# A recurrent attention layer on one core: the maximum subtracted by TensorE, half a of a softmax ahead of half b, and another order at the lead-in

## The chip, the cores and the metric

The kernel runs on one core of a Trainium2 chip. A core has TensorE (PE in the profile; its weight loads are PEld), VectorE (DVE), ScalarE (ACT), GpSimd (POOL) and SyncE (SP), which issues most DMAs. The metric is the device time of one execution in microseconds (us), as the median over several runs.

## The reference

Four layers in the order A, B, A, B, each as `x = x + layer(layernorm(x))`, on 2048 tokens of width 640 in bf16. The change touches layer B alone, a recurrence over 64 segments of 32 tokens with 8 memory tokens, 32 heads of 128:

```python
for s in range(n_seg):                                   # 64 steps, each needs the memory of the one before
    h = jnp.concatenate([mem, xs], axis=1)               # 8 memory rows + 32 tokens
    q, k, v = h @ Wq, h @ Wk, h @ Wv                     # per head, 32 heads of 128
    scores = jnp.where(mask, q @ k.T * scale, -1e9)      # causal among tokens, memory seen by all
    p = softmax(scores)
    o = (p @ v) @ Wo                                     # summed over the heads
    mem = o[:, :8]                                       # the next step's memory
    outs.append(o[:, 8:])
```

## The kernel before

Layer A and layer B follow each other, twice. Everything said here is of `layer_B` (L804). Its instructions are recorded at one line, L113, a wrapper (`_OrdNC`) that chains the instructions of each of TensorE, ScalarE, VectorE and GpSimd in the order of the code: the order written by hand is the order that runs. DMAs go out on SP in the order of the code as well, with eight semaphores in rotation, so that an issue waits for the landing of the eighth before it.

**Rows.** In one step the 32 rows of interest are 24 tokens and the 8 memory rows. `HX` holds their transposed columns; the 24 token columns come from a LayerNorm and a transpose (`ln_spread`, PSUM tile `lntps`) for four steps at a time, and the 8 memory columns are written at the end of the step before, from `MT`. The other 8 tokens of each segment (the "tail") do not depend on the memory; their projections (`TX`, `tail_unit`, `vtail_unit`) are made for four steps at a time and fill TensorE while the recurrence waits. `TK`, `TQ` (tiles `b_tK`, `b_tQ`) hold their K and Q, `VTd` in DRAM their V.

**One step** (from L1086). TensorE makes Ka, Qa, Kb, Qb with `by_head` (20 matmuls of 512 columns, four column tiles at a time; Qb as two passes of 256, `b_Qb` and `b_Qc`). Heads 0 to 15 are half a, 16 to 31 half b. ScalarE copies each to SBUF (`kq`), VectorE transposes (`turn`) into `KT` and `QT`. A mask group starts the PSUM tile of the scores (`mask_mm`, four matmuls of an identity with the mask), `scores` adds 32 small matmuls of a half. Then the softmax: `soft_max` (negated maximum), `soft_sub`, `soft_exp` on ScalarE, `soft_sum`, `soft_rec`, `soft_p` (on GpSimd), and `p_turn` transposes into `PTa` or `PTb`. Va and Vb (`thin_mm`, five chunks of four matmuls each) lie beside it on TensorE. Then come a part of a deferred output product (`OPSd`, from `OTdef`), the tail unit, in some steps `lntps`, then `pv` for half a and half b (PSUM tiles `b_OTP`), evacuated to `OTsb`; two chunks of `vtail`; the output product `OPS` (64 matmuls with the eight tiles `wo`, in the order 0, 4, 1, 5, 3, 7, 2, 6); another part of `OPSd`, `vtail`, and the next memory through `msb` and `MT` into `HX`.

**PSUM.** Five buffers `ps` in rotation, and the pool `po` with one buffer for each of its tags (`tail`, `ops`, `opsd`).

**The lead-in** of a layer B (L996 to L1028) lies at the end of layer A. `load_B_wo` issues the eight `wo` loads on SP, and the dependency with `C.rows` puts layer A's last row stores behind the load with k = 6. Four tail units follow, each with its evacuation and its transpose on VectorE (`tail_turn`, into `b_tK` and `b_tQ`), then the memory: five matmuls into `mt0` and a copy into `HX`, on VectorE too. In SBUF the pools of layer B take the addresses that layer A's tiles leave.

Of the kernel before, what the change touches and what calls it, by code (L numbers as in the profile page):

```python
# [28 lines left out]
D = 640  # L29
# [735 lines left out]
            out_stage_b(nseg - 1, tt)  # L765


class BWeights:
    pass

# [33 lines left out]
def layer_B(nc, tc, C, W, x_src, xb_src, x_dst, mem0, B_Wv, B_Wo, nsteps=64, out_bf16=False, tag=""):  # L804
# [6 lines left out]
    with ExitStack() as ctx:  # L811
        def pool(name, bufs):
            return ctx.enter_context(tc.tile_pool(name=name, bufs=bufs, reuse_waits="tile"))
# [4 lines left out]
        bx = pool("b_x", 1)  # L818
        sml = pool("b_sml", 2)
        kqp = pool("b_kqp", 4)  # L820
        wop = pool("b_wo", 1)
        W.wo = [wop.tile([128, 4, D], BF16, name=f"b_wo{k}") for k in range(7)]
        W.wo.append(pool("b_wo7", 1).tile([128, 4, D], BF16, name="b_wo7"))
        st = pool("b_state", 1)
        w2 = pool("b_w2", 2)
        wk = pool("b_wk", 1)
        sm = pool("b_sm", 2)

# [6 lines left out]
        def ps_tile(shape, dtype, name):  # L835
            return pp.tile(shape, dtype, name=name, tag="ps")
# [2 lines left out]
        Pn = st.tile([128, 2, 5, 64], BF16, name="b_Pn")  # L839
        mask5, selm = C.mask5, C.selm  # L840
        QZ = st.tile([128, 32, 32], BF16, name="b_QZ")
        OTdef = [wk.tile([128, 32, 32], BF16, name=f"b_OTdef{i}") for i in range(2)]

        def init_state():
            XO_ = bx.tile([64, 320], F32, name="b_XO", tag="XO")
            nc.vector.memset(XO_[:], 0.0)
            XOd_ = bx.tile([64, 320], F32, name="b_XOd", tag="XOd")
            nc.vector.memset(Pn[:], 0.0)
            nc.vector.memset(QZ[:], 0.0)
            return XO_, XOd_  # L850
# [4 lines left out]
        def evac(eng, dst, src, scale=None):  # L855
            if eng == "act":
                if scale is None:
                    nc.scalar.copy(dst, src)
                else:
                    nc.scalar.activation(out=dst, in_=src, func=ACT.Copy, scale=scale)  # L860
            else:
                if scale is None:
                    nc.vector.tensor_copy(dst, src)
                else:
                    nc.vector.tensor_scalar(out=dst, in0=src, scalar1=scale, scalar2=None, op0=ALU.mult)
# [27 lines left out]
        def ln_spread(key, ps=None):  # L893
            kind, g = key
            xt = ln_xt.pop(key)
            tps = ps or ps_tile([128, NCH, 4, 32], BF16, "b_lntps")
            for c in range(NCH):
                nc.tensor.transpose(tps[:, c, :, :].rearrange("p i t -> p (i t)"), xt[:, 128 * c:128 * c + 128], C.identb[:])
            if kind == "H":
                HX[g] = hp.tile([128, NCH, 4, 32], BF16, name="b_HX", tag="HX")  # L900
                nc.scalar.copy(HX[g][:, :, :, 0:24], tps[:, :, :, 0:24])
            else:
                TX[g] = tx.tile([128, NCH, 16, 8], BF16, name="b_TX", tag="TX")
                nc.scalar.copy(TX[g][:].rearrange("p c s t -> p c (s t)"), tps[:].rearrange("p c i t -> p c (i t)"))
# [14 lines left out]
        def by_head(cols_ap, Wt, h0, nh, ps):  # L919
            for c in range(NCH):  # L920
                wt = Wt[:, c, 128 * h0:128 * (h0 + nh)].rearrange("p (h e) -> p h e", e=128)
                for j in range(4):
                    nc.tensor.matmul(ps[32 * j:32 * j + 32, :].rearrange("p (h x) -> p h x", x=32), lhsT=cols_ap[:, c, :], rhs=wt[:, :, 32 * j:32 * j + 32],
                                     start=(c == 0), stop=(c == NCH - 1), tile_position=(0, 32 * j), skip_group_check=True)
            return ps
# [4 lines left out]
        def tails_copy(s):  # L930
            g, i = divmod(s, 4)
            KT[s] = wk.tile([128, 32, 40], BF16, name="b_KT", tag="KT")
            for t_, dst in ((TQ, QZ[:, :, 0:8]), (TK, KT[s][:, :, 32:40])):
                nc.gpsimd.tensor_copy(dst, t_[g][:, :, 8 * i:8 * i + 8])
# [11 lines left out]
        def tail_unit(g, k, ps):  # L946
            proj, b = divmod(k, 2)
            return by_head(tail_cols(g), W.wq if proj else W.wk, 16 * b, 16, ps)

        def tail_evac(k, ps):  # L950
            sb = kqp.tile([128, 512], BF16, name="b_tu", tag="kq")
            evac("act", sb[:], ps[:], SCB if k // 2 else None)
            return sb

        def tail_turn(g, k, sb):
            proj, b = divmod(k, 2)
            T_, nm = ((TK, "b_tK"), (TQ, "b_tQ"))[proj]
            if b == 0:
                T_[g] = w2.tile([128, 32, 32], BF16, name=nm, tag=nm)
            nc.vector.transpose(out=T_[g][:, 16 * b:16 * b + 16, :], in_=sb[:].rearrange("p (h x) -> p h x", x=32))  # L960
# [37 lines left out]
        m0 = bx.tile([8, D], BF16, name="b_m0", tag="XOd")  # L998
        nc.sync.dma_start(m0[:], mem0)
        load_B_wv(nc, W, B_Wv)  # L1000
        for k in range(8):
            f = load_B_wo(nc, W, B_Wo, k)
            if k == 6:
                for r in C.rows:
                    tc.add_manual_dep(r.ins, f.ins.name, mybir.DependencyInfo(mybir.DependencyClass.NoSync, mybir.DependencyReason.SCHED_ONLY), reason="order")
        ln_begin(("T", 0), C.after)
        ln_end()
        ln_begin(("H", 0))
        ln_spread(ln_ready.pop(0))
        for k in range(4):  # L1010
            ps = tail_unit(0, k, ps_tile([128, 512], F32, "b_tail"))
            if k == 0:
                ln_end()
                XO, XOd = init_state()
            tail_turn(0, k, tail_evac(k, ps))
        ln_spread(ln_ready.pop(0))
        mt0 = ps_tile([128, NCH, 8], F32, "b_MT0")
        for c in range(NCH):
            nc.tensor.matmul(mt0[:, c, :], lhsT=m0[:, 128 * c:128 * c + 128], rhs=C.identb[0:8, 0:8], start=True, stop=True)
        nc.vector.tensor_copy(HX[0][:, :, 0, 24:32], mt0[:])  # L1020
        tails_copy(0)
        VT[0] = wk.tile([128, 2, 512], BF16, name="b_VT", tag="VT")
        for k in range(4):
            ps = vtail_unit(0, k)
            evac("dve" if k % 2 else "act", VT[0][:, k // 2, 256 * (k % 2):256 * (k % 2) + 256], ps[:])
        for j in range(4):
            nc.sync.dma_start(VTd[1:4].rearrange("s t (b n e) -> (s t) n b e", b=2, e=512)[:, j, :, :], VT[0][32 * j + 8:32 * j + 32, :, :])

# [52 lines left out]
        for s in range(nsteps):  # L1081
# [33 lines left out]
                            nc.tensor.matmul(SP[32 * j:32 * j + 32, 0 if tail else 1 + i, :], lhsT=lhsT, rhs=KT[s][:, h, :],  # L1115
                                             start=False, stop=True, tile_position=(0, 32 * j), skip_group_check=True)

            negmax = sm.tile([128, 2, 5], F32, name="b_negmax", tag="negmax")
            ssum = sm.tile([128, 2, 5], F32, name="b_ssum", tag="ssum")
            rs = sm.tile([128, 2, 5], F32, name="b_rs", tag="rs")  # L1120
            E_ = wk.tile([128, 2, 5, 40], BF16, name="b_E", tag="E0")
# [2 lines left out]
                nc.vector.tensor_reduce(out=negmax[:, b, :], in_=SP[:], axis=AX.X, op=ALU.max, negate=True)  # L1124

            def soft_sub(b, SP):
                nc.vector.tensor_tensor(out=SP[:], in0=SP[:], in1=negmax[:, b, :].unsqueeze(2).to_broadcast([128, 5, 40]), op=ALU.add)

            def soft_exp(b, SP):
                nc.scalar.activation(out=E_[:, b], in_=SP[:], func=ACT.Exp)  # L1130
# [29 lines left out]
                    vps = vtail_unit(work[0], work[1], vc, min(NCH, vc + n_), vps)  # L1160
                    vc = min(NCH, vc + n_)

            VH[s] = wk.tile([128, 2, 512], BF16, name="b_Vth", tag="Vth")
            for b in range(2):
                for nm, Wt, D_, scale in (("K", W.wk, KT, None), ("Q", W.wq, QT, SCB)):
                    if b and nm == "Q":
                        for e, q in enumerate((ps_tile([128, 256], F32, "b_Qb"), po.tile([128, 256], F32, name="b_Qc", tag="tail"))):
                            by_head(cols, Wt, 16 + 8 * e, 8, q)
                            turn(kq(q, scale, 256), D_, 16 + 8 * e, 8)
                    else:  # L1170
                        ps = by_head(cols, Wt, 16 * b, 16, ps_tile([128, 512], F32, f"b_{nm}{'ab'[b]}"))
                        turn(kq(ps, scale), D_, 16 * b, 16)
            SPa = mask_mm(0)
            Va = thin_mm(cols, W.wv, 0, "b_Va", 0, 1)
            scores(0, SPa)
            thin_mm(cols, W.wv, 0, "b_Va", 1, 3, Va)
            SPb = mask_mm(1)
            thin_mm(cols, W.wv, 0, "b_Va", 3, 4, Va)
            scores(1, SPb)
            thin_mm(cols, W.wv, 0, "b_Va", 4, NCH, Va)  # L1180
            PTa = wk.tile([128, 2, 4, 40], BF16, name="b_PTa", tag="PTa")
            PTb = wk.tile([128, 2, 4, 40], BF16, name="b_PTb", tag="PTb")
            soft_max(0, SPa)
            soft_sub(0, SPa)
            soft_exp(0, SPa)
            soft_max(1, SPb)
            soft_sub(1, SPb)
            soft_sum(0)
            soft_rec(0)
            soft_p(nc.gpsimd, 0)  # L1190
            soft_exp(1, SPb)
            evac("act", VH[s][:, 0, :], Va[:])
            soft_sum(1)
            soft_rec(1)
            soft_p(nc.gpsimd, 1)
            p_turn(0, PTa)
            p_turn(1, PTb)
            Vb = thin_mm(cols, W.wv, 1, "b_Vb")
            evac("act", VH[s][:, 1, :], Vb[:])
            if not last:  # L1200
                od_chunk(0)
# [13 lines left out]
            otf = [ps_tile([128, 2, 4, 40] if j else [128, 4, 40], F32, "b_OTP") for j in range(4)]  # L1215
            ots = {j: (otf[j][:, 0, :, :], otf[j][:, 1, :, :]) for j in (1, 2, 3)}
            ots[0] = [otf[0][:], None]
            OTsb = wk.tile([128, 32 * 40], BF16, name="b_OTsb", tag="OTsb")
            OTv = OTsb[:].rearrange("p (a x) -> p a x", a=2)
            pv(0, PTa, ots)  # L1220
            evac("dve", OTv[:, 0, 0:160], otf[0][:].rearrange("p i c -> p (i c)"))
# [156 lines left out]
```

## Time and profile before

| | |
|---|---|
| median of three runs | 2438.76 us (2437.13 to 2443.8) |
| the profiled execution: its time, its span | 2441.25 us, 2439.1 us |
| granted TensorE clock, mean over the span | 0.993 |
| TensorE, weight loads | 2296.4 us (94%), 1507.5 us (62%) |
| VectorE, ScalarE, GpSimd | 1882.4, 1414.9, 749.2 us |
| first `Ka` of the two layers B | 360.15 and 1580.78 us |
| a step of layer B, median of 90 without and 36 with `lntps` | 13.19 and 13.24 us |
| the first step of each layer B | 15.95 and 14.93 us |

The times of instructions come from the profiled execution, and "busy" is the time in which an engine has an instruction in work. A row of a group gives line, engine, operation, output<-input by the names of the program, the tile shapes, the count, then busy us, mean ns of one, and the idle time ahead of them with what ended most of it. A row of the timeline gives start, duration of the whole stretch (all its instructions together), engine, line, and in brackets an idle time with what ended it. Durations of matmuls include their pipeline, so the spacing of the groups gives their cost.

### The profile page before, as it was taken

What the parts mean: (1) busy time and instruction counts of PE and PEld (TensorE: products, weight loads), DVE (VectorE), ACT (ScalarE), POOL (GpSimd) and SP (SyncE); (2) the same over time, 40 slices, a digit from 0 to 9 for tenths busy, and PEclk for the clock granted to TensorE, in tenths of its full rate; (3) what the DMA queues carried; (4) which work ended last, traced back from release to release, by engine and by line L of the source; (5) the groups of instructions that cost most, each with busy time, mean ns of one, the idle gap of its engine ahead of it and who ended that gap; (6) DMA issues with size and microseconds to landing.
All of it is one profiled execution on the core that took longest, in us unless ns stands there. A gap on an engine that the chain in (4) does not pass through costs nothing.

```text
span 2439.1 us, 139382 instructions
## 1 busy us (share of the span) xinstructions
PE 2296.4 (94%) x62322; PEld 1507.5 (62%) x62386; DVE 1882.4 (77%) x4699; ACT 1414.9 (58%) x3194; POOL 749.2 (31%) x1589
## 2 busy tenths in 40 slices
PE   8999989999999999999889999899999999999998
PEld 5566656666666666666555666566666666666665
DVE  8999857777777777777679998577777777777776
ACT  6999954444454444444369899544444544444443
POOL 5677631111111111111146776311111111121111
PEclk9999999999999999999999999999999999999999
DMA  4121271111111111111220111711111111111110
GB/s 166 49 82 62 70 258 24 28 32 29 31 29 30 30 30 31 30 31 27 66 86 18 66 40 37 270 23 26 28 27 29 28 25 27 27 29 26 29 24 19
DMA packets 168883, 123.38 MB, mean 51 GB/s; under 512 B 104652, under 2 KB 153180, under 8 KB 166492
## 3 DMA queue, kind: packets, MB, share of 16 engines
q1 hardware_dynamic: 167288, 112.69, 16.1%
q8 instruction: 487, 7.98, 1.4%
q10 hardware_dynamic: 996, 1.79, 0.2%
q14 instruction: 112, 0.92, 0.1%
HBM read 79.60 MB, written 34.80 MB: 47 GB/s over the span
## 4 chain that ended last, share of the span: by engine, by line
PE 66%; DVE 15%; ACT 10%; DMA 4%; issue 2%; POOL 1%; SPq 1%; ACTq 0%; DVEq 0%; POOLq 0%
PE b_OPS L113 11%; PE b_Ka L113 6%; PE b_Qa L113 5%; PE b_Kb L113 5%; DVE a_nm L142 4%; ACT a_PT L142 4%; PE b_Va L113 4%; PE b_Vb L113 4%; PE b_tail L113 4%; PE b_vtail L113 3%; PE a_S L113 3%; PE b_OTP L113 2%; PE b_OPSd L113 2%; PE b_SP L113 2%; PE b_Qb L113 2%
## 5 line engine op out<-in xcount | busy, mean ns | idle before, releaser
L113 PEld LDWEIGHTS <-b_HX 128*32 128x32 bf16 x17920 | 466.4, 96 | 287.4 <-DVE b_HX L113 17.4
L113 POOL TENSOR_TENSOR b_Pn<-b_E,b_rs 128x200 bf16<-128x200 bf16 x256 | 133.5, 522 | 1096.4 <-DVE b_rs L113 1078.5
L142 DVE TENSOR_REDUCE a_nm<-a_S 128x2 f32<-128x512 f32 (+3 forms) x512 | 395.4, 817 | 54.6 <-PE a_S L113 39.1
L142 ACT ACTIVATE a_PT<-a_T 128x1024 bf16<-128x1024 f32 (+1 forms) x384 | 345.9, 905 | 28.7 <-PE a_T L113 21.8
L113 PE MATMUL b_OPS<-b_wo,b_OTsb 128*32 128x320 bf16 x8192 | 307.0, 301 | 4.5 <-DVE b_OTsb L113 4.5
L113 PEld LDWEIGHTS <-b_OTsb 128*32 128x32 bf16 x8192 | 207.4, 97 | 74.7 <-DVE b_OTsb L113 27.0
L113 DVE STREAM_TRANSPOSE b_KT<-b_kq 128x512 bf16<-128x512 bf16 x256 | 181.3, 708 | 84.6 <-ACT b_kq L113 83.9
L142 POOL TENSOR_SCALAR_AFFINE_SELECT a_PT<-a_PT 128x256 bf16<-128x256 bf16 x380 | 188.5, 501 | 158.3 <-ACT a_PT L142 157.0
L113 ACT ACTIVATE b_E<-b_SP 128x200 bf16<-128x200 f32 x256 | 86.3, 337 | 235.1 <-DVE b_SP L113 224.1
L113 PE MATMUL b_Va<-b_wv,b_HX 128*32 128x512 bf16 x2560 | 221.9, 381 | 0.0
L113 DVE STREAM_TRANSPOSE b_QT<-b_kq 128x256 bf16<-128x256 bf16 (+1 forms) x384 | 183.9, 504 | 39.9 <-ACT b_kq L113 36.5
L113 DVE CAST b_HX<-b_MT 128x16 bf16<-128x16 f32 (+1 forms) x380 | 65.0, 172 | 185.7 <-PE b_MT L113 177.5
L113 ACT CAST b_msb<-b_OPS 128x64 bf16<-128x64 f32 x378 | 69.3, 256 | 210.9 <-PE b_OPS L113 210.9
L113 PE MATMUL b_Ka<-b_wk,b_HX 128*32 128x512 bf16 x2560 | 165.1, 385 | 14.6 <-DVE b_HX L113 14.4
L113 PEld LDWEIGHTS <-b_TX 128*32 128x32 bf16 x5360 | 143.5, 96 | 55.6 <-issue 2.8
L113 DVE CAST b_OTsb<-b_OTP 128x160 bf16<-128x160 f32 (+1 forms) x384 | 133.9, 376 | 43.7 <-PE b_OTP L113 39.4
L113 PE MATMUL b_Qa<-b_wq,b_HX 128*32 128x512 bf16 x2560 | 162.6, 383 | 0.0
L113 PE MATMUL b_Vb<-b_wv,b_HX 128*32 128x512 bf16 x2560 | 162.3, 379 | 0.0
L113 PE MATMUL b_Kb<-b_wk,b_HX 128*32 128x512 bf16 x2560 | 161.5, 381 | 0.0
L113 ACT CAST b_kq<-b_Ka 128x512 bf16<-128x512 f32 x128 | 74.9, 585 | 133.6 <-PE b_Ka L113 133.6
L113 PE MATMUL b_vtail<-b_wv,b_TX 128*32 128x256 bf16 x2680 | 148.8, 273 | 1.2 <-issue 1.2
L113 ACT CAST b_OTsb<-b_OTP 128x320 bf16<-128x320 f32 x256 | 96.5, 429 | 82.2 <-PE b_OTP L113 81.1
(186 smaller groups left out, 5049.5 us busy)
## 6 DMA issues: line engine op xcount, KB each, us to landing
b_wv<-in_B_Wv_dram SPq DMA_DIRECT2D x10, 1024.0 KB
b_wo<-in_B_Wo_dram SPq DMA_DIRECT2D x16, 640.0 KB
b_VT<-b_VTd SPq DMA_DIRECT2D x504, 16.0 KB
b_XO<-xres SPq DMA_DIRECT2D x256, 30.0 KB
b_VTd<-b_vt SPq DMA_DIRECT2D x480, 16.0 KB
b_xt<-xres_bf SPq DMA_DIRECT2D x40, 160.0 KB
b_wk<-in_B_Wk_dram SPq DMA_DIRECT2D x20, 256.0 KB
b_wq<-in_B_Wq_dram SPq DMA_DIRECT2D x20, 256.0 KB
```

The costliest lines, as they stand in the source:

```text
L113: r = f(*a, **k)
L142: r = f(*a, **k)
```

## The change

1. `soft_sub` is four matmuls (slices of the identity with the negated maximum broadcast over 40 columns) that add into the PSUM tile of the scores; `negmax` is bf16.
2. Qb is one pass of 512 columns in a `ps` buffer. Its transpose follows `soft_max` of half a on VectorE.
3. On TensorE, scores a follow mask a at once; then three chunks of Va, the subtraction of half a, the rest of Va, mask b, scores b, two chunks of Vb, the subtraction of half b, the rest of Vb. On VectorE, sum a and reciprocal a stand ahead of maximum b, and the transpose of `PTa` ahead of sum b. The product P of half b is made by VectorE.
4. At the lead-in, five `wo` loads stand ahead of layer A's last row stores and the other three behind later loads. The copy of the memory stands ahead of the four transposes of the tail units, and `init_state` behind them. ScalarE makes all four evacuations of V.
5. The pools are laid out anew: `b_w2` and `b_state` ahead of `wo`, `wo` in two pools, and `OTdef`, `Vth`, `PTa`, `PTb`, `OTsb` in a pool `b_wkl`.

```diff
+WO_FIRST, WO_LAST = (0, 4, 1, 5, 3), (7, 2, 6)
...
-        wop = pool("b_wo", 1)
-        W.wo = [wop.tile([128, 4, D], BF16, name=f"b_wo{k}") for k in range(7)]
-        W.wo.append(pool("b_wo7", 1).tile([128, 4, D], BF16, name="b_wo7"))
+        w2 = pool("b_w2", 2)
         st = pool("b_state", 1)
-        w2 = pool("b_w2", 2)
+        W.wo = [None] * 8
+        for nm, ks in (("b_wo", WO_FIRST), ("b_wol", WO_LAST)):
+            p_ = pool(nm, 1)
+            for k in ks:
+                W.wo[k] = p_.tile([128, 4, D], BF16, name=f"b_wo{k}")
+        wkl = pool("b_wkl", 1)
         wk = pool("b_wk", 1)
...
-        for k in range(8):
+        for k in WO_FIRST + WO_LAST:
             f = load_B_wo(nc, W, B_Wo, k)
-            if k == 6:
+            if k == WO_FIRST[-1]:
...
         ln_spread(ln_ready.pop(0))
+        tsb = []
         for k in range(4):
             ps = tail_unit(0, k, ps_tile([128, 512], F32, "b_tail"))
+            tsb.append(tail_evac(k, ps))
             if k == 0:
                 ln_end()
-                XO, XOd = init_state()
-            tail_turn(0, k, tail_evac(k, ps))
...
         nc.vector.tensor_copy(HX[0][:, :, 0, 24:32], mt0[:])
+        for k in range(4):
+            tail_turn(0, k, tsb[k])
+        XO, XOd = init_state()
...
-            evac("dve" if k % 2 else "act", VT[0][:, k // 2, ...], ps[:])
+            evac("act", VT[0][:, k // 2, ...], ps[:])
...
-            negmax = sm.tile([128, 2, 5], F32, name="b_negmax", tag="negmax")
+            negmax = sm.tile([128, 2, 5], BF16, name="b_negmax", tag="negmax")
...
             def soft_sub(b, SP):
-                nc.vector.tensor_tensor(out=SP[:], in0=SP[:], in1=negmax[:, b, :].unsqueeze(2).to_broadcast([128, 5, 40]), op=ALU.add)
+                for j in range(4):
+                    nc.tensor.matmul(SP[32 * j:32 * j + 32], lhsT=C.identb[:, 32 * j:32 * j + 32], rhs=negmax[:, b, :].unsqueeze(2).to_broadcast([128, 5, 40]),
+                                     start=False, stop=True, tile_position=(0, 32 * j), skip_group_check=True)
...
+                    ps = by_head(cols, Wt, 16 * b, 16, ps_tile([128, 512], F32, f"b_{nm}{'ab'[b]}"))
+                    sbs = kq(ps, scale)
                     if b and nm == "Q":
-                        for e, q in enumerate((ps_tile([128, 256], F32, "b_Qb"), po.tile([128, 256], F32, name="b_Qc", tag="tail"))):
-                            by_head(cols, Wt, 16 + 8 * e, 8, q)
-                            turn(kq(q, scale, 256), D_, 16 + 8 * e, 8)
+                        qb = sbs
                     else:
-                        ps = by_head(cols, Wt, 16 * b, 16, ps_tile([128, 512], F32, f"b_{nm}{'ab'[b]}"))
-                        turn(kq(ps, scale), D_, 16 * b, 16)
+                        turn(sbs, D_, 16 * b, 16)
             SPa = mask_mm(0)
-            Va = thin_mm(cols, W.wv, 0, "b_Va", 0, 1)
             scores(0, SPa)
-            thin_mm(cols, W.wv, 0, "b_Va", 1, 3, Va)
-            SPb = mask_mm(1)
-            thin_mm(cols, W.wv, 0, "b_Va", 3, 4, Va)
-            scores(1, SPb)
-            thin_mm(cols, W.wv, 0, "b_Va", 4, NCH, Va)
             soft_max(0, SPa)
+            turn(qb, QT, 16, 16)
+            Va = thin_mm(cols, W.wv, 0, "b_Va", 0, 3)
             soft_sub(0, SPa)
             soft_exp(0, SPa)
-            soft_max(1, SPb)
-            soft_sub(1, SPb)
+            thin_mm(cols, W.wv, 0, "b_Va", 3, NCH, Va)
+            SPb = mask_mm(1)
+            scores(1, SPb)
             soft_sum(0)
             soft_rec(0)
             soft_p(nc.gpsimd, 0)
+            soft_max(1, SPb)
+            evac("act", VH[s][:, 0, :], Va[:])
+            Vb = thin_mm(cols, W.wv, 1, "b_Vb", 0, 2)
+            soft_sub(1, SPb)
             soft_exp(1, SPb)
-            evac("act", VH[s][:, 0, :], Va[:])
+            thin_mm(cols, W.wv, 1, "b_Vb", 2, NCH, Vb)
+            p_turn(0, PTa)
             soft_sum(1)
             soft_rec(1)
-            soft_p(nc.gpsimd, 1)
-            p_turn(0, PTa)
+            soft_p(nc.vector, 1)
             p_turn(1, PTb)
-            Vb = thin_mm(cols, W.wv, 1, "b_Vb")
             evac("act", VH[s][:, 1, :], Vb[:])
```

## The prediction

> **What bounds the kernel now.** I read the page first: the shares by engine, then the chain that ended last.
>
> ```profile
> PE 2296.4 (94%) x62322; PEld 1507.5 (62%) x62386; DVE 1882.4 (77%) x4699; ACT 1414.9 (58%) x3194; POOL 749.2 (31%) x1589
> PE 66%; DVE 15%; ACT 10%; DMA 4%; issue 2%; POOL 1%; SPq 1%; ACTq 0%; DVEq 0%; POOLq 0%
> ```
>
> TensorE is busy for 94% of the span and carries two thirds of the chain. A wait that disappears from another engine is therefore worth little unless TensorE stands for it, and anything added to TensorE is suspect. The list of waits says who stands where (summed us, count, mean us):
>
> ```profile
> ACT b_E L113 <- DVE b_SP L113: 224.1, 248, 2.3
> PE b_Ka L113 <- DVE b_HX L113: 14.4, 4, 7.7
> PE b_OTP L113 <- DVE b_PTb L113: 10.3, 33, 0.6
> ```
>
> ScalarE's 224 us before the exponentials is idle time of an engine that has time. TensorE itself waits inside the softmax only at its end (the P·V matmuls of half b, on `PTb`), and twice for long at a lead-in (`Ka` on `HX`). Next, the timeline of a step without a LayerNorm transpose; its first `Ka` matmul is at 735.53, and all offsets below count from there (start, us, engine):
>
> ```profile
> 735.53 1.26 PE L113 MATMUL b_Ka<-b_wk,b_HX 128*32 128x512 bf16 x20
> ...
> 739.87 0.26 PE L113 MATMUL b_SP<-b_mask,c_identb 128*32 128x200 bf16 x4
> ...
> 741.47 0.38 DVE L113 TENSOR_TENSOR b_SP<-b_SP,b_negmax 128x200 f32<-128x200 f32 x1
> 741.59 1.27 PE L113 MATMUL b_Vb<-b_wv,b_HX 128*32 128x512 bf16 x20
> ...
> 743.71 0.57 DVE L113 STREAM_TRANSPOSE b_PTa<-b_Pn 128x256 bf16<-128x256 bf16 x2
> 744.29 0.57 DVE L113 STREAM_TRANSPOSE b_PTb<-b_Pn 128x256 bf16<-128x256 bf16 x2
> 744.33 0.20 PE L113 MATMUL b_OTP<-b_PTa,b_Vth 32*128 32x40 bf16 x4
> ...
> 744.79 0.33 DVE L113 CAST b_OTsb<-b_OTP 128x160 bf16<-128x160 f32 x1
> 745.01 0.20 PE L113 MATMUL b_OTP<-b_PTb,b_Vth 32*128 32x40 bf16 x4 [0.30 <-ACT b_tu L113]
> 745.32 0.40 PE L113 MATMUL b_vtail<-b_wv,b_TX 128*32 128x256 bf16 x8
> ```
>
> From `Ka` to the end of the tail unit (8.49) TensorE never stands. Then P·V a starts at 8.80, just after `PTa` ends (8.75), and P·V b at 9.48, 0.15 after `PTb` ends (9.33). The steps last 13.19 us (median of 90 without `lntps`) and 13.24 (36 with it). A step with `lntps`, whose `Ka` is at 709.15, has no such slack:
>
> ```profile
> 717.75 0.45 PE L113 MATMUL b_lntps<-c_identb,b_xt 128*128 128x128 bf16 x5
> 718.14 0.20 PE L113 MATMUL b_OTP<-b_PTa,b_Vth 32*128 32x40 bf16 x4
> 718.60 0.32 DVE L113 CAST b_OTsb<-b_OTP 128x160 bf16<-128x160 f32 x1
> 718.97 0.40 PE L113 MATMUL b_vtail<-b_wv,b_TX 128*32 128x256 bf16 x8
> ```
>
> P·V a follows TensorE's own work there (8.99). `vtail` takes the PSUM buffer that the CAST empties, so it comes 0.83 to 0.84 after P·V a (9.83).
>
> **The step, part by part.** *The maximum on TensorE.* Two DVE subtractions of 0.375 go. Two groups of four 128x200 matmuls come; the mask group before is the same form, and the next group starts 0.09 after it (739.87, 739.96): +0.18 on TensorE.
>
> *Q b in one pass.* The 512 columns cost what twice 256 cost (1.08 each by the spacing of the groups): nothing. But half b's `QT` now needs one ScalarE cast of 0.60 and one DVE transpose of 0.71 in place of two halves that overlap.
>
> *Scores b.* Q b ends at 4.33, its cast ends at 5.20, `QT` b runs 5.24 to 5.95 (max a stands ahead of it, 4.86 to 5.23, behind `KT` b). TensorE meanwhile does mask a and scores a (to 4.64), Va (1.08), subtraction a, mask b: to 5.92. Scores b can start at 6.01: +0.09 waited.
>
> *Subtraction b.* Subtraction a is over at 5.40, ScalarE starts 0.27 later (as the CAST does behind P·V a, 718.34 to 718.60) and exp a, 0.34, ends at 6.01; DVE does sum a and rec a (6.04 to 6.60) ahead of max b (6.55 to 6.92), so subtraction b starts at 6.98. TensorE has finished scores b at 6.23 and two of the five chunks of Vb at 6.67: +0.31 waited. Were max b free of the two, it would still take 0.18 until the last score is out of the array, 0.37 for the reduction and 0.10 for two hand-overs, less 0.44 of cover: 0.21. The eight `Vb` matmuls of 0.055 are the whole cover, and behind the waiting matmul stand the rest of Vb, OPSd and the tail unit, which need no softmax at all. I charge both waits in full because every group of matmuls in the timeline stands in the order of the code. The Trainium skill ("TensorE: Matmul & The Clock Gate", step by step) says that only weight loads are pulled ahead and matmuls keep their order, which speaks against this change; if matmuls could overtake, 0.18 alone would be added. No row of before decides that alone.
>
> *Half a ahead of half b.* `PTa` ends about 7.87 in place of 8.75. Half b's chain: exp b 7.34 to 7.68, then `PTa`, sum b, rec b, P b on DVE (0.38 by the subtraction's row, POOL took 0.522), `PTb` 8.80 to 9.37, P·V b not before 9.52. So `PTb` hardly comes earlier than now: DVE wins 0.75 of subtractions and gives back 0.38 and the wait on TensorE.
>
> *Sum.* TensorE reaches the P·V stage 0.18 + 0.09 + 0.31 = 0.58 later: 9.07, and 9.19 with the 0.12 that the change of matmul form takes now. Without `lntps` P·V a goes 8.80 to 9.19 and `vtail` 9.19 + 0.84 = 10.03 in place of 9.79: +0.24, as slack absorbs 0.34. With `lntps` nothing absorbs it: P·V a 9.57, `vtail` 10.41, +0.57. So 90 x 0.24 + 36 x 0.57 = 42.1, and 0.6 for the two last steps: +42.7 us. Bounds for TensorE's addition are 0.43 (no wait on `QT`, 0.25 on the maximum) and 0.68 (0.1 more in hand-overs): steps +0.09 and +0.41, or +0.34 and +0.66, so +23 to +55.
>
> **The two lead-ins.** Here the change removes a wait. The first:
>
> ```profile
> 357.52 1.30 DVE L113 STREAM_TRANSPOSE b_tK<-b_tu 128x512 bf16<-128x512 bf16 x2 [4.02 <-DMA xres<-a_xnew]
> ...
> 359.94 0.16 DVE L113 CAST b_HX<-b_MT 128x40 bf16<-128x40 f32 x1
> 360.15 0.62 PE L113 MATMUL b_Ka<-b_wk,b_HX 128*32 128x512 bf16 x4 [5.48 <-DVE b_HX L113]
> ```
>
> The CAST that `Ka` needs stands behind four transposes, whose targets lie in memory that layer A's last row stores still read. TensorE idles 5.5 us here and 7.7 in the second lead-in. Ahead of the transposes, and with their targets moved, the CAST needs only its matmuls: `Ka` starts when `vtail` ends, 354.7 and 1573.2. The windows show what else goes (PEclk is third from the end):
>
> ```profile
> 354.70:360.00 5.30, 0.00 (x0) 0.00 (x0) 2.48 (x5) 0.00 (x0) 0.00 (x0) 0.93 0.88 285
> 360.20:366.30 6.10, 6.10 (x60) 2.25 (x64) 1.98 (x4) 1.18 (x2) 0.74 (x2) 0.52 0.18 40
> ```
>
> After the idling the granted clock is 0.52 for 6.1 us. The first steps take 15.95 and 14.93 where a usual one takes 13.19: 2.8 and 1.7 more. The gain is 5.5 + 2.8 + 7.7 + 1.7 = 17.7 us. The Trainium skill (same page, what is actually happening) has half clock until one busy window of 3.4 us: as an estimate from it 1.7 us a lead-in, and 16.6 in all; the row of 6.1 us is longer, so the rows decide. Three weights (`wo` 7, 2, 6, 640 KB each) now queue on SP behind `b_xt`, `XOd` and `XO`. The first of them is used by the sixth of the eight groups of the first OPS, 10.0 + 1.4 us after `Ka`, at 366 and 1584.6; at the 285 GB/s of the window their 1.9 MB take 6.9 us, to about 361 and 1583. The TensorE work of the first step is the cover; without it each late us is paid. ScalarE takes two evacuations from DVE (0.37 each) under the step's start: nothing.
>
> Net: 42.7 - 17.7 = +25.0. The profiled execution took 2441.25 us (span 2439.1), so 2466.3; it lies 2.5 above the median of the three runs, so against 2438.76: **2464 us**.
>
> **Rivals.**
> *A, the end of softmax still ends the step (faster).* If the two new waits together stay under 0.16, TensorE comes at most 0.34 late, P·V b still waits for `PTb` (9.52 against 9.48), and the 90 steps lose nothing; 36 lose 0.18 to 0.34, 6.5 to 12. Net -11 to -5: 2428 to 2433, likeliest 2430. For it: `PTb` is what P·V b waits for now. Against: max b behind the long `QT` b, sum a and rec a, all in rows above. This is also the result if a waiting matmul lets others pass.
> *B, the lead-ins win nothing (slower still).* The late weights or the stores hold the first OPS by some 9 us in each lead-in: +42.7 is left, 2481. For: the DMA share is 0.88. Against: 11 us of TensorE work in between.
> *C, the two parts cancel.* The steps cost only 11 to 25 us, at or below the low bound, the lead-ins give 17.7: 2432 to 2446.
>
> **How the numbers follow.** The forecast has 0.66, A 0.17, B 0.08, C 0.09. The forecast's own range is 2464 with the steps' bounds and a lead-in gain of 13 (no help from the clock) to 18: 2444 to 2481. The range of 8 in 10 takes in C and B with a little over: 2436 to 2486; what lies outside is A and the low end of C. Some 0.3%, 7.3 us, is what a measurement can tell from no change. Faster: most of A, 0.14. Within: the rest of A and C, 0.12. Slower: the forecast and B, 0.74.
>
> **What would show it.** Right: steps of about 13.43 and 13.81; `vtail` 10.03 and 10.41 after `Ka`; new rows of waits of TensorE's `b_SP` on `b_negmax` (about 40 us) and on `b_QT` (about 11); no row of ScalarE waiting for DVE's `b_SP`; `Ka` at 354.7 with a granted clock near 1.0 and first steps near 13.4. Wrong: subtraction b starts within 0.1 of the second Vb chunk, or P·V b still waits for `PTb` in most steps (A); OPS of the first steps waits for a DMA (B).

## The result, and the profile after

The changed kernel takes 2466.3 us (median of four runs, 2463.69 to 2470.78) beside 2437.95 us; the ratio is 1.0108, 95% interval 1.0092 to 1.0125. The forecast was 2464. The profiled execution took 2463.69 us with a span of 2462.0, 22.9 more than the span before.

The page after, shares by engine and the chain:

```profile
PE 2340.5 (95%) x60850; PEld 1470.0 (60%) x60850; DVE 1829.7 (74%) x4439; ACT 1431.8 (58%) x3070; POOL 683.4 (28%) x1461
PE 69%; DVE 16%; ACT 9%; issue 3%; DMA 3%; SPq 1%; POOL 0%; ACTq 0%; DVEq 0%; POOLq 0%
```

VectorE gave up 53 us of work and TensorE took on 44 us of busy time. TensorE's share of the chain rose from 66% to 69%. The waits of TensorE in layer B (summed us, count, longest us; the prediction calls the third column a mean, which it is not, but no step of its sum uses it as one):

```profile
PE b_SP L113 <- DVE b_negmax L113: 11.1, 58, 0.4
PE b_Ka L113 <- DVE b_HX L113: 4.6, 5, 1.6
...
PE b_OTP L113 <- issue: 3.9, 2, 2.3
PE b_OTP L113 <- DVE b_PTb L113: 2.4, 8, 0.3
```

The wait for `PTb` has gone from 10.3 to 2.4 us, the one at the lead-ins from 14.4 to 4.6, and a wait for the maximum has come in their place. The trace before has 55 more waits of the P·V matmuls that the prediction's list leaves out, put down to the copy that ends together with `PTb`; they are gone too:

```profile
PE b_OTP L113 <- ACT b_tu L113: 16.5, 55, 0.3
```

A step without `lntps`, `Ka` at 749.78:

```profile
754.69 0.37 DVE L113 TENSOR_REDUCE b_negmax<-b_SP 128x5 bf16<-128x200 f32 x1
754.97 0.71 DVE L113 STREAM_TRANSPOSE b_QT<-b_kq 128x512 bf16<-128x512 bf16 x1
755.11 0.27 PE L113 MATMUL b_SP<-b_negmax,c_identb 128*32 128x200 bf16 x4
...
755.95 0.63 PE L113 MATMUL b_Vb<-b_wv,b_HX 128*32 128x512 bf16 x8
...
756.35 0.33 DVE L113 TENSOR_REDUCE b_negmax<-b_SP 128x5 bf16<-128x200 f32 x1
756.73 0.27 PE L113 MATMUL b_SP<-b_negmax,c_identb 128*32 128x200 bf16 x4
756.82 0.83 PE L113 MATMUL b_Vb<-b_wv,b_HX 128*32 128x512 bf16 x12
...
758.61 0.57 DVE L113 STREAM_TRANSPOSE b_PTb<-b_Pn 128x256 bf16<-128x256 bf16 x2
758.93 0.20 PE L113 MATMUL b_OTP<-b_PTa,b_Vth 32*128 32x40 bf16 x4
```

Two chunks of Vb cost 0.44 by their spacing, so the subtraction of half b could stand at 756.39 and stands at 756.73, right behind the reduction: 0.34 lost. The bar of the Vb matmuls (0.63) hides half of that, since it includes the pipeline; the profile counts only 21.9 us of idle time ahead of all the subtraction's matmuls, where the spacing ahead of half b alone gives about 0.34 x 126 = 43. P·V a comes at offset 9.15. In a step with `lntps` (`Ka` at 763.12) it comes at 9.53:

```profile
772.65 0.20 PE L113 MATMUL b_OTP<-b_PTa,b_Vth 32*128 32x40 bf16 x4
...
773.49 0.40 PE L113 MATMUL b_vtail<-b_wv,b_TX 128*32 128x256 bf16 x8
```

Where the 22.9 us come from, by the first `Ka` of each step in both traces (us):

| | before | after | difference |
|---|---|---|---|
| start to the first `Ka` | 360.15 | 352.91 | -7.2 |
| first steps of the two layers | 15.95, 14.93 | 15.62, 16.20 | +0.9 |
| last `Ka` of the first layer B to first of the second | 378.19 | 369.53 | -8.7 |
| the other 2 x 62 steps | 1651.0 | 1687.6 | +36.6 |
| last step and the rest | | | +1.2 |

The 88 steps without `lntps` among them went from 13.19 to 13.44 in the median (mean 13.31 to 13.48), the 36 with it from 13.24 to 13.72 (mean 13.33 to 13.93).

Not all of the first and third row belongs to the change. In the trace before, TensorE's granted clock was 0.50 for 3.4 us in the midst of each layer A, from 116.9 and from 1396.9 us (first fence; the columns are us, then busy us of PE, PEld, DVE, ACT, POOL, then clock, DMA share, GB/s). The trace after has full clock there (second fence) and runs 1.6 and 1.4 us further ahead from there on, in code that the change does not touch:

```profile
116.90:120.30 3.40, 3.18 (x16) 1.33 (x13) 2.86 (x5) 2.17 (x4) 3.00 (x8) 0.50 0.20 62
```

```profile
116.90:120.30 3.40, 3.25 (x36) 1.67 (x35) 3.40 (x7) 3.14 (x6) 3.01 (x8) 1.00 0.22 71
```

Why the clock fell there is not known; the traces of other runs have such a stretch at other places of layer A, or none. Without these 3.0 us the traces are 25.8 us apart, and the ratio of the run times gives 26.

### The profile page after: what moved, and what is told of

Read it like the earlier page. It is cut to its first block, busy times and chain, and to the rows that moved or that the text cites. A ratio compares the mean times of both kernels' runs of the same rounds, so it can differ in the third digit from the quotient of the medians.

```text
span 2462.0 us, 135749 instructions
## 1 busy us (share of the span) xinstructions
PE 2340.5 (95%) x60850; PEld 1470.0 (60%) x60850; DVE 1829.7 (74%) x4439; ACT 1431.8 (58%) x3070; POOL 683.4 (28%) x1461
## 4 chain that ended last, share of the span: by engine, by line
PE 69%; DVE 16%; ACT 9%; issue 3%; DMA 3%; SPq 1%; POOL 0%; ACTq 0%; DVEq 0%; POOLq 0%
PE b_OPS L113 11%; PE b_Ka L113 6%; PE b_Kb L113 5%; PE b_Qa L113 5%; PE b_Qb L113 5%; PE b_tail L113 5%; DVE a_nm L142 5%; PE b_vtail L113 4%; ACT a_PT L142 4%; PE b_SP L113 4%; PE b_Va L113 3%; PE b_Vb L113 3%; PE b_OPSd L113 3%; PE a_S L113 3%; PE b_OTP L113 2%
## 5 line engine op out<-in xcount | busy, mean ns | idle before, releaser
L113 PEld LDWEIGHTS <-b_HX 128*32 128x32 bf16 x15360 | 385.2, 96 | 277.8 <-DVE b_HX L113 7.2
L113 POOL TENSOR_TENSOR b_Pn<-b_E,b_rs 128x200 bf16<-128x200 bf16 x128 | 66.8, 522 | 985.6 <-ACT b_Vth L113 897.6
L113 PEld LDWEIGHTS <-b_OTsb 128*32 128x32 bf16 x8192 | 236.7, 97 | 44.0 <-DVE b_OTsb L113 7.7
L113 PEld LDWEIGHTS <-c_identb 128*32 128x32 bf16 (+1 forms) x3032 | 155.4, 96 | 176.4 <-issue 103.5
L113 DVE STREAM_TRANSPOSE b_QT<-b_kq 128x512 bf16<-128x512 bf16 x256 | 180.8, 706 | 37.9 <-ACT b_kq L113 34.0
L113 PEld LDWEIGHTS <-b_TX 128*32 128x32 bf16 x5360 | 151.3, 96 | 62.8 <-issue 0.8
L113 PE MATMUL b_Vb<-b_wv,b_HX 128*32 128x512 bf16 x2560 | 186.9, 380 | 0.0
L113 PE MATMUL b_Va<-b_wv,b_HX 128*32 128x512 bf16 x2560 | 180.2, 380 | 0.0
L113 PE MATMUL b_Qb<-b_wq,b_HX 128*32 128x512 bf16 x2560 | 160.6, 379 | 0.0
```

Of the source, the lines that this page charges most:

```text
L113: r = f(*a, **k)
```

## The experiments

**The lead-in alone.**

The change without its items 1 to 3: everything from `negmax` on in the diff above is taken back, among it

```diff
-            thin_mm(cols, W.wv, 1, "b_Vb", 2, NCH, Vb)
...
-            p_turn(0, PTa)
             soft_sum(1)
             soft_rec(1)
-            soft_p(nc.vector, 1)
+            soft_p(nc.gpsimd, 1)
+            p_turn(0, PTa)
             p_turn(1, PTb)
+            Vb = thin_mm(cols, W.wv, 1, "b_Vb")
```

> The new lead-in, pools and order of the weights, with the step as it was before (subtraction on VectorE, Qb in two passes, old order, both products P on GpSimd). My theory: the change is the sum of a gain at the two lead-ins (about 15 us by the trace after: first Ka 7.2 and 8.7 us earlier, the first steps about as long as before) and a loss in the steps. So 2438 - 15 = 2423 us, ratio 0.994, steps at 13.19 and 13.24, first Ka at 352.9. Rival: the lead-in wins nothing by itself and the steps cost only what the total shows, 28 us: then about 2438.

Measured: ratio 0.9965 (0.9953 to 0.9976), some 8 us less than before; first `Ka` at 352.75, gap 367.97, first steps 16.19 and 16.22, the other steps 13.22 and 13.23. The lead-in gains by itself, so the rival falls, but by the run times it gains little more than half of the 15 us expected. The traces show where the rest went. First `Ka`, gap and first steps are 16 us shorter than before, but 3.0 of these are the clock in layer A, which is 1.00 there in this trace too. The 124 other steps sum to 4 us more than before, in single long steps (15 of them above 13.6 us, where before has 12); in five of the 15 TensorE stands for 0.3 us or more at what the profile calls `issue`, which is explained under the run without the late weights. That leaves about 9 us. Against this kernel the changed step costs 1.0108/0.9965 = 1.0144, 35 us.

**More cover ahead of the subtraction of half b.**

```diff
-            Vb = thin_mm(cols, W.wv, 1, "b_Vb", 0, 2)
+            Vb = thin_mm(cols, W.wv, 1, "b_Vb", 0, 4)
             soft_sub(1, SPb)
             soft_exp(1, SPb)
-            thin_mm(cols, W.wv, 1, "b_Vb", 2, NCH, Vb)
+            thin_mm(cols, W.wv, 1, "b_Vb", 4, NCH, Vb)
```

> The changed kernel with four chunks of Vb, in place of two, ahead of the subtraction of half b. My theory: TensorE's wait for the maximum of half b (0.28 in every step) is what the steps pay beyond the slack. The subtraction comes at about 7.04 in place of 6.95, nothing waits for it, TensorE reaches P V a at 8.84 in place of 9.15, P V b stays on PTb at 9.5; steps 13.22 and 13.44 in place of 13.44 and 13.72, so 90 x 0.22 + 36 x 0.28 = 30 us less: 2436, ratio 0.999. Rival: half b's chain on VectorE (sum, reciprocal, P, PTb) sets the step already, the wait on TensorE is hidden: 2466, or more as exp b comes 0.1 later.

Measured: ratio 1.0037 (1.0023 to 1.0051), 17 us less than the changed kernel where 30 were expected. P·V a came at 8.81 in place of 9.15, as worked out, and the wait moved on:

```profile
PE b_OTP L113 <- DVE b_PTb L113: 33.1, 88, 0.6
```

88 waits for `PTb` in place of 8: half b's chain on VectorE now ends the step (P·V b at 9.54). Steps took 13.34 and 13.47; the second is as expected, the first loses 0.1 more than I gave it. The wait on TensorE was real and worth something, and close behind it stood a second bound.

**The same, with P of half b on GpSimd again.**

```diff
-            soft_p(nc.vector, 1)
+            soft_p(nc.gpsimd, 1)
```

> The run with four chunks of Vb ahead of the subtraction of half b, and the product P of half b on GpSimd (0.522 and two hand-overs) in place of VectorE (0.38). My theory: with the wait on TensorE gone, half b's chain to PTb ends the steps without lntps (P V b at 9.54, waiting on PTb in most steps), so 0.25 to 0.3 longer is paid there nearly in full and less with lntps: 88 x 0.25 + 36 x 0.07 = 25 us more than with VectorE, ratio 1.014. Rival: TensorE's own work still ends the steps there: 1.0037 as it was.

Measured: ratio 1.0137 (1.0115 to 1.0159), where 1.014 was expected; 122 waits for `PTb`, 66.4 us in all. That half b's chain is the bound there is shown.

**The subtraction back on VectorE, the rest as changed.**

```diff
-                for j in range(4):
-                    nc.tensor.matmul(SP[32 * j:32 * j + 32], ...)
+                nc.vector.tensor_tensor(out=SP[:], in0=SP[:], in1=negmax[:, b, :]..., op=ALU.add)
```

> The changed kernel with the subtraction back on VectorE (two of 0.375 us per step, f32 maximum), everything else as changed. My theory: TensorE loses its 0.18 of matmuls and its wait, but VectorE's chain, which is as long as TensorE's in the changed order, gets 0.75 longer and sub a stands behind QT b: PTb ends at about 10.2 in place of 9.4, P V b 10.3, vtail 10.6: steps +0.55 without lntps and +0.25 with it, 58 us more: 2524, ratio 1.035. Rival: the matmuls on TensorE are the whole loss: then 0.49 less per step where it counts, about 2420 to 2440.

Measured: ratio 1.0322 (1.0307 to 1.0338). The wait tells why:

```profile
PE b_OTP L113 <- DVE b_PTb L113: 109.2, 120, 1.1
```

In the new order the subtraction on VectorE is worse: TensorE's matmuls save 2% there. So the matmuls are not what is wrong with the change.

**Maximum b ahead of sum a and reciprocal a.**

```diff
+            soft_max(1, SPb)
             soft_sum(0)
             soft_rec(0)
             soft_p(nc.gpsimd, 0)
-            soft_max(1, SPb)
```

> The changed kernel with maximum b ahead of sum a and reciprocal a on VectorE, nothing else. My theory: TensorE's wait shrinks by 0.1 (subtraction b at 6.85 in place of 6.95, the floor being scores b, the reduction and two hand-overs), but VectorE stands idle from 5.95 until the scores of half b are there and everything behind (sum a, P a, PTa, sum b, P b, PTb) comes 0.6 to 0.7 later: P V b at 10.2 in place of 9.55, steps +0.45 without lntps, +0.2 with it: 47 us more, 2510 to 2520, ratio 1.030. Rival: only TensorE's wait counts: 0.1 x 124 = 12 us less, ratio 1.006.

Measured: ratio 1.0351 (1.0336 to 1.0367), a little more than expected. The subtraction of half b moved from 6.95 to 6.86 in the steps with `lntps`, as worked out, and P·V b from 9.55 to 10.2 or 10.3, waiting for `PTb` 125 times. In this order neither place of maximum b is good: half b's scores come 0.34 later than before (5.95 in place of 5.61), and either VectorE waits for them ahead of half a's work, or TensorE waits behind that work. How much of these 0.34 comes from Qb in one pass, and how much from Va ahead of them, no run separates.

**The subtraction on TensorE in the old order.** Lead-in as in the first experiment, maxima back to back as before (the main lines against that experiment; the comments are not in the code, and the later line of Vb goes):

```diff
             soft_max(0, SPa)
             soft_sub(0, SPa)          # four matmuls, behind the last chunk of Va
             soft_exp(0, SPa)
             soft_max(1, SPb)
+            Vb = thin_mm(cols, W.wv, 1, "b_Vb", 0, 2)
             soft_sub(1, SPb)          # four matmuls
+            thin_mm(cols, W.wv, 1, "b_Vb", 2, NCH, Vb)
```

> The new lead-in with the old order of the step (Qb in two passes, maximum b right behind maximum a, P b on GpSimd), but the subtraction as four matmuls on TensorE: of half a behind the last chunk of Va, of half b behind two chunks of Vb. My theory: the matmuls alone cost 0.18 where TensorE is the bound, and the loss of the change is the order on VectorE (sum a and reciprocal a ahead of maximum b, with too little cover). Here the maxima end at 5.91 and 6.28, both subtractions find them ready, PTb ends about 0.13 earlier: steps without lntps -0.13, with it +0.18, so 88 x -0.13 + 36 x 0.18 = -5 us against the lead-in alone: ratio 0.9945. Rival: the subtraction on TensorE is itself the loss (hand-overs between the engines included): steps +0.2 to +0.3 in all, +30 us, ratio 1.009.

Measured: ratio 0.9927 (0.9912 to 0.9943), faster than both kernels and, a little more than the 0.9945 expected, than the lead-in alone. Steps 13.08 and 13.39 in the median, against 13.22 and 13.23 of the lead-in alone: -0.14 and +0.16, worked out as -0.13 and +0.18. A step with `Ka` at 888.56:

```profile
894.39 0.41 PE L113 MATMUL b_Va<-b_wv,b_HX 128*32 128x512 bf16 x4
894.62 0.27 PE L113 MATMUL b_SP<-b_negmax,c_identb 128*32 128x200 bf16 x4
894.66 0.37 DVE L113 TENSOR_REDUCE b_negmax<-b_SP 128x5 bf16<-128x200 f32 x1 [0.19 <-PE b_SP L113]
894.70 0.62 PE L113 MATMUL b_Vb<-b_wv,b_HX 128*32 128x512 bf16 x8
...
895.14 0.27 PE L113 MATMUL b_SP<-b_negmax,c_identb 128*32 128x200 bf16 x4
```

The subtraction of half b stands 0.44 behind the start of Vb: no wait. The same eight `Vb` matmuls are enough cover here, because the reduction starts with Vb (894.66 and 894.70), where in the changed kernel it starts 0.40 later (756.35 and 755.95).

**TensorE's subtraction only where there is slack.**

```diff
+            on_dve = bool(ln_ready)
...
             def soft_sub(b, SP):
+                if on_dve:
+                    nc.vector.tensor_tensor(out=SP[:], in0=SP[:], ...)
+                    return
                 for j in range(4):
```

> The version with the old order and the subtraction on TensorE, but in the 36 steps with a LayerNorm transpose the subtraction stays on VectorE. My theory: with lntps TensorE has no slack before P V a, so the 0.18 of matmuls are paid in full there (13.39 against 13.23), and are hidden, with an earlier PTb, in the others (13.08 against 13.22). So 36 x 0.16 = 6 us less than with TensorE everywhere: ratio 0.990, steps 13.08 and 13.23. Rival: the steps with lntps are longer for what the step before or the transpose itself brings: no difference, ratio 0.9927.

Measured: ratio 0.9897 (0.988 to 0.9915), steps 13.04 and 13.23. `ln_ready` is true in the steps that make `lntps`; the maximum is f32 there. By ratio that is 7 us less than with TensorE everywhere, though the two intervals overlap a little; by the steps the 0.16 is won back. It is the lowest ratio of this study.

**Without the late weights.**

```diff
         for k in WO_FIRST + WO_LAST:
+            if k in WO_LAST:
+                W.wo[k] = W.wo[WO_FIRST[WO_LAST.index(k)]]
+                continue
             f = load_B_wo(nc, W, B_Wo, k)
```

> The changed kernel without the loads of the three late weights: output products of the head groups 7, 2 and 6 use the tiles 0, 4 and 1, so those products are left out and others stand in their place. My theory: TensorE's stalls inside the first steps (2.3 us, and 1.6 + 1.2 us with a clock of 0.67 after) come from these three transfers, which fill the DMA queues until the first P V and beyond; without them the first steps take about 13.5 in place of 15.6 and 16.2, 4.8 us less: 2461, ratio 1.009. Rival: the stalls come from the first pass through the step's code whatever the queues carry: first steps 15.6 and 16.2 as they are, 2466.

The kernel leaves out three of the eight weights: their products use tiles 0, 4 and 1. Measured: ratio 1.0057 (1.004 to 1.0075), 12 us less than the changed kernel (5 were expected), and first steps of 13.28 and 13.18. By the traces the first steps give 5.4 us, about as expected; the other 4.7 us of their difference lie between the layers and in the other steps, and their cause is not shown. That the three transfers lengthen the first steps is shown. What they do there is seen in the changed kernel's own trace: TensorE stands within one group of P·V b, whose other matmuls of the same inputs have run, and the row says `issue`: it waits for nothing that the profile shows.

```profile
365.05 0.19 PE L113 MATMUL b_OTP<-b_PTb,b_VT 8*128 8x40 bf16 x1 [2.29 <-issue]
```

```profile
1593.85 0.19 PE L113 MATMUL b_OTP<-b_PTb,b_VT 8*128 8x40 bf16 x2 [1.57 <-issue]
```

The windows (us, PE, PEld, DVE, ACT, POOL, clock, DMA share, GB/s) show the queues full when the stall begins, and empty at that time in the kernel without these loads (second fence):

```profile
361.00:363.00 2.00, 1.47 (x79) 0.77 (x71) 1.55 (x7) 1.04 (x3) 0.00 (x0) 1.00 1.03 350
363.00:365.00 2.00, 0.00 (x0) 0.00 (x0) 1.19 (x3) 0.31 (x1) 0.00 (x0) 1.00 0.30 84
```

```profile
361.00:363.00 2.00, 1.70 (x92) 1.02 (x84) 1.59 (x6) 1.04 (x3) 0.00 (x0) 1.00 0.01 2
```

What TensorE stands for is its own code, and the packets of the trace show it. The page has a queue of instructions:

```profile
q8 instruction: 476, 7.80, 1.3%
```

These are 476 packets of 16 KB, about one for each 256 of TensorE's 121,700 matmuls and weight loads. The first stall ends at 365.05 with TensorE's 9667th instruction of the trace, the second at 1593.85 with one 60,927 further on, which is 238 x 256 less one. All eleven traces together have 90 such stalls of 0.3 us or more in their layers B; within one layer of one trace all stand at the same place modulo 256, to within two instructions, and each ended 1.2 to 1.6 us after a 16 KB packet had landed. Usually such a packet starts when some 250 instructions are left before the place at which it is needed. In the changed kernel the one for the first stall started at 362.56, with 9 left, and landed at 363.70; without the late weights the same packet started at 359.87, with 181 left, landed at 361.08, and TensorE passed the place at 362.63 without a stop. So the weights, which fill the queues, hold up the code, and the missing code holds up TensorE.

**The weights issued earlier.** On the lead-in alone, the memset of XO ahead of the four transposes:

```diff
+        XO = bx.tile([64, 320], F32, name="b_XO", tag="XO")
+        nc.vector.memset(XO[:], 0.0)
         for k in range(4):
             tail_turn(0, k, tsb[k])
-        XO, XOd = init_state()
+        XO, XOd = init_state(XO)
```

> The new lead-in with the old step, as in the run of the lead-in alone, and the memset of XO moved ahead of the four tail transposes, so that the load of XO and behind it the three late weights go out at about 352.4 in place of 354.6. My theory: the stalls inside the first steps (first steps of 16.2 us, where 13.2 came without the late weights) are the tail of that transfer; 2.2 us earlier takes about 2 us from each first step: first steps about 14.2, 4 us less than the lead-in alone, ratio 0.995. Rival: the queue is full until layer A's row stores have landed, an earlier issue only waits there: first steps 16.2 as before, ratio 0.9965.

Measured: ratio 0.9954 (0.9937 to 0.997), which does not tell the theory from the rival; the first steps do. They took 17.60 and 15.34, together no less than the 16.19 and 16.22 of the lead-in alone, and TensorE's stall in P·V b is 2.40. The first of the three loads went out at 353.3, about a microsecond earlier and not two, and the three took SP 4.64 us, in place of 2.29 in the changed kernel. TensorE's code packet started at 363.01 and landed at 363.89. An earlier issue on SP was not an earlier end of the transfers, so my theory fails here. The rival's result stands; its reason, layer A's row stores, is not shown.

## Why the prediction was right

The sign, the place and the mechanism of the step were right. The total, 2464 for 2466.3, is closer than the sum deserves: the steps were forecast at +42.7 and measure +37.8 (with the last two), the lead-ins at -17.7 and measure about -12, so the two errors of some 5 us cancelled by luck.

*The step.* TensorE's addition was forecast as 0.58 and measures 0.54 (the tail unit at 7.95 in place of 7.41). Of its three terms, the matmuls came out as worked out, the wait for the maximum at 0.34 for 0.31, and the wait of scores b for `QT` at 0.03 for 0.09: `QT` b ended at 755.68, offset 5.90, and scores b started at 5.95, 0.11 behind mask b, which takes 0.09 anyway. `vtail` came at 10.07 and 10.37 for 10.03 and 10.41. Slack was absorbed where forecast: +0.25 and +0.48 in the medians for +0.24 and +0.57. The sum goes by the means, though. The steps with `lntps` cost 36 x 0.60 = 21.6 for 20.5; the others cost 88 x 0.17 = 15.0 for 21.6 (of 90 steps). So the term that was too large is the step without `lntps`: before, the mean of these steps lies 0.12 above their median, after only 0.04; why is not shown.

*That waits are paid in full* is shown: with the wait taken away by cover, P·V a came 0.34 earlier, and nothing had been moved but the order of Vb and the subtraction. In the changed kernel no matmul behind the waiting one ran before it. This is what the Trainium skill ("TensorE: Matmul & The Clock Gate", step by step) says of the order of matmuls.

*Rival A* named the right second bound. Its condition, less than 0.16 of waits, did not hold in the changed kernel (0.34 and 0.03). The run with cover meets it, and there P·V b does wait for `PTb` in most steps; but the steps take 13.34 without `lntps` and 13.47 with it, 0.15 and 0.23 more than before, where A had nothing and 0.18 to 0.34. Without `lntps`, P·V b then stands at 9.54, 0.06 later than before, and `vtail` at 9.89, 0.10 later; the ratio is 1.0037 and not below 1.

*The lead-ins.* `Ka` started 7.2 and 8.7 us earlier in its stretch, for 5.5 and 7.7. Of this 1.6 and 1.4 are the half clock in layer A of the trace before, which is also why `vtail` itself ended earlier (352.9, not 354.7): the changed kernel is 1.6 us ahead from 120 us on, long before the first `wo` load. So 5.6 and 7.3 belong to the lead-ins, about as forecast. But the first steps did not get shorter: 15.62 and 16.20 for about 13.4. The step that failed is the one on the late weights. I let them land at 361 and be needed at 366, and took TensorE's work in between as their cover. DMA ran full until 363, and the stall came not at OPS, where the weights are used, but before, in P·V b, for code that came behind them. In the first lead-in the clock stayed at 1.00, but the stall of 2.29 us took that gain, and in the second a stall of 1.57 us brought the half clock back. So of the 4.5 us for the clock nothing was left. A mechanism near rival B's was there, late weights that hold TensorE, at somewhat over a quarter of its price. In all the lead-ins gave 15.0 for 17.7 by the traces, and 12.0 without the clock in layer A.

*The row I said to look for* is smaller than forecast (11.1 us for 40), although the loss is there: it has to be read from the spacing of the groups. The row of `b_SP` on `b_QT`, forecast as about 11, has a single wait of 1.0 us, as this term was nearly nothing.

## What to carry to other kernels

Moving a small operation to the engine that is the bound can pay: four matmuls that cost 0.09 us together replaced 0.375 us on a chain. But a matmul that waits holds everything queued behind it, so put it behind as much independent work as its operand takes to arrive, counted from the producer's own place in its engine's order; here two chunks were enough with the maxima back to back and 0.34 us short with two small operations ahead of the second. Where steps differ in slack, decide step by step which engine does the work. When a transfer is moved to a place where nothing needs it yet, ask what else goes through the full queues: here it was TensorE's own code. And before a gain is credited to a change, compare the two traces in the stretches that it does not touch.

## What the runs showed of the hardware

Short stalls can be followed by a loss of clock: in the changed kernel's second lead-in TensorE stood for 0.29 and 1.57 us between 1591.8 and 1593.9, and from 1594 to 1598 the granted clock was 0.67 in the mean, so that OPS took 3.54 us in place of 2.35. In the first lead-in a stall of 2.29 us was followed by a clock of 1.00 (365 to 368); what decides between the two is not shown. I had reckoned with this only behind the 5 to 8 us of the old lead-ins; the Trainium skill ("TensorE: Matmul & The Clock Gate", what is actually happening) gives an idle window of about 3.4 us, and this trace shows half clock after less.

Transfers of weights alone stopped TensorE in the middle of a group of matmuls whose operands were ready, for 1.6 to 2.7 us in the traces shown here (2.66 with four chunks of cover), well before the weights were used: TensorE's code came in packets of 256 instructions, and with the queues full the next packet started with 9 instructions left in place of 181. The profile shows such a wait as `issue`, and a count of instructions modulo 256 tells it.
